# The main PSUM banks as four tiles in place of two tiles of two banks, with new tables for the first and the last batches

## The chip, the cores and the metric

The kernel runs on one core of one Trainium2 chip. The metric is the device time of one execution in microseconds (us), the median of three runs. A core has five engines that work side by side and meet at semaphores: TensorE (PE; its weight loads are shown as PEld), VectorE (DVE), ScalarE (ACT), GpSimd (POOL) and SyncE (SP, which here issues the DMAs).

## The reference

The input is attention-like data of 8 batches, 8 heads, 576 positions and 64 features per head. Each batch goes through a decaying linear attention (retention) and then a gated feed-forward block with a spatial mixing matrix.

```python
scores = scale * (q @ k^T)
ret = (scores * Dmat) @ v                    # Dmat: gamma_h ** (i - j) for i >= j, else 0
x = ret, heads side by side                  # (8, 576, 512)
h = max(x @ w_in, 0); u, v = halves of h     # (8, 576, 512) each
v_n = (v - mean) / sqrt(var + 1e-6)          # over the last axis
v_s = w_spatial @ v_n + b_spatial            # over the 576 positions
out = (u * v_s) @ w_out
```

## The kernel before

Everything is unrolled and runs in an order written out by hand. The kernel is a set of generators ("chains"), one for each small piece of work, such as a product, its eviction from PSUM and the additions that follow. Three strings, `ORDER` (lines 41 to 87), `STEADY` (lines 88 to 110) and `LAST` (lines 111 to 127), list the chains by name; each time a name stands there, that chain is advanced by one step. Each engine receives its instructions in the order in which the steps are traced (`keep_in_program_order`), so that every engine's queue is in order, and only semaphore waits shift the queues against each other.

`ORDER` is played once: it loads and splits the weights (`w`), does batches 0 and 1, and starts on batches 2 and 3. `STEADY` is played five times, for a = 2 to 6, and each time finishes batch a while it works on the retention of batches a+1 and a+2. `LAST` is played once for batch 7. Names in the tables that the text below speaks of: `w` splits a piece of a weight into a high and a low part, and its two letters say whether POOL (p) or DVE (v) does the second and the last step; `p` updates the retention state; `A` makes summed weight blocks; `W` and `Y` are one block product each (6 matmuls for one PSUM bank), followed by one or two additions on DVE or a copy on ACT; `y`, `X`, `F`, `U`, `V`, `G` are whole products (12 to 14 matmuls); `v` with a last number of 4 handles the remaining 64 rows.

PSUM has eight banks. Four belong to the retention (`r0` and `r1`, two banks each). The other four serve all the main products. They are two tiles, `m0` and `m1`, of two banks each. The string `BANKS` (line 128) gives the bank of each next product, digit k being half k % 2 of tile k // 2: banks 0 and 1 lie in `m0`, banks 2 and 3 in `m1`. The waits are put in by the framework from the accesses of each tile. In the program before, a matmul that starts in bank 0 waits for every earlier read of `m0`, thus also for a read of bank 1, its neighbour; and a read of bank 0 waits for the matmuls that were traced ahead of it into bank 1. The other tile's banks put no such wait on it. `weight` (from line 376) also uses a bank, as scratch for integer operations on DVE.

`pair_chain` (from line 900) and its table name `Q` take a whole two-bank tile at once; no table names `Q`.

All the engines' instructions are recorded through one helper, so that the profile gives line 175 for nearly all of them; they are told apart by their tiles: `m<-slot,wout` is a matmul into a main bank, from activations and the output weight, `o<-m,o` on DVE reads a main bank and adds it to a result.

Of the kernel before, what the change touches and what calls it, by code (L numbers as in the profile page):

```python
# [46 lines left out]
    w.1.0.vp g.0.2 w.0.0.vp p.0.2.pp v.0.0 p.0.1.pp w.1.2.vv w.1.1.vp b.0.1 w.0.0.vp p.0.2.pp p.0.2.pp d.1.0 v.0.0 S
    d.1.0 w.1.3.vp g.0.2 b.0.2 w.1.2.vv w.0.0.vp v.0.1 w.0.1.vp w.0.1.vp w.0.0.vp b.0.2 k.0.3.p t.0.p b.0.2 w.0.2.vp
    d.1.1 p.0.2.pp p.0.2.pp b.0.2 w.0.1.vp q.0.3.v g.0.3 s.0.p p.0.3.pp p.0.3.pp S d.1.1 t.0.p p.0.3.pp b.0.2 v.0.1
    w.0.0.vp w.0.2.vp d.1.0 p.0.3.pp v.0.1 b.0.2 S t.0.p g.0.3 v.0.0 v.0.0 v.0.1 w.0.1.vp w.0.2.vp v.0.1 b.0.3 v.0.0  # L50
    w.0.1.vp w.0.2.vp v.0.1 g.1.0 s.1.p d.1.1 g.1.0 b.0.3 s.2.p v.0.1 b.0.3 b.0.3 e.0.p D.0.3 v.0.0 v.0.2 b.0.3
    v.0.1 w.0.1.vp w.0.0.vp v.0.2 k.1.0.p v.0.2 s.1.p S v.0.2 b.0.3 p.1.0.vp v.0.0 e.0.p w.0.2.vp k.1.1.p w.0.3.vv
    v.0.0 q.1.0.p v.0.1 w.0.2.vp p.1.0.vp v.0.4 s.5.p s.2.p v.0.4 q.1.1.p w.0.3.vv v.0.0 v.0.4 v.0.1 p.1.0.vp v.0.3
    v.0.3 D.2.1 e.0.p p.1.0.vp v.0.4 v.0.0 s.3.p s.3.p d.1.2 v.0.3 p.1.0.vp v.0.2 b.1.0 w.0.3.vv b.1.0 v.0.2 g.1.1
    p.1.1.pv b.1.0 v.0.2 D.2.0 d.1.2 d.1.2 w.0.3.vv v.0.4 b.1.0 w.0.3.vv s.0.p D.2.2 U.1 v.0.2 T.1 s.4.p s.5.p v.0.4
    d.1.3 s.4.p p.1.1.pv v.0.3 v.0.2 g.1.1 v.0.4 U.1 v.0.3 p.1.1.pv v.0.4 k.1.2.p v.0.2 b.1.0 v.0.4 U.0 V.0.0 b.1.0
    U.0 p.1.1.pv V.0.0 v.0.3 v.0.4 w.0.2.vp b.1.1 b.1.1 v.0.3 g.1.2 V.0.0 b.1.1 w.0.1.vp b.1.1 p.1.2.vp v.0.4 v.0.4
    v.0.3 q.1.2.p v.0.3 v.0.4 v.0.3 w.0.3.vv d.2.0 v.1.0 p.1.1.pv v.1.0 p.1.2.vp w.0.3.vv v.1.0 w.2.0.pv p.1.2.vp
    g.1.2 b.1.1 v.1.0 V.0.0 V.0.0 w.2.0.pv w.2.1.vp v.1.0 d.2.0 p.1.2.vp b.1.1 d.1.3 V.0.0 V.1.0 b.1.2 b.1.2
    w.2.0.pv w.2.1.vp V.0.3 D.2.3 V.0.3 g.1.3 V.1.0 t.1.p q.1.3.p w.2.1.vp b.1.2 b.1.2 V.1.2 w.2.0.pv w.2.1.vp  # L60
    w.2.1.vp p.1.2.vp d.1.3 V.0.1 V.0.1 w.2.0.pv w.2.2.vp k.1.3.v w.2.0.pv v.1.0 A.0.0.v A.0.1.p t.1.p V.1.2
# [24 lines left out]
    K.2.4.vv F.1.1.1 F.1.1.2
# [25 lines left out]
    v.a.4 v.a.4 W.a.0.1 v.a.4 W.a.0.2.p W.a.1.1 W.a.1.1 W.a.0.2.p W.a.0.1 W.a.0.6 W.a.0.6 W.a.0.7 W.a.0.2.p v.a.4  # L112
    W.a.0.7 W.a.0.5 W.a.0.5 W.a.0.5 W.a.0.3 W.a.1.2.p v.a.4 W.a.0.4 W.a.0.3 W.a.0.4 W.a.1.2.p v.a.2 W.a.1.6 W.a.1.6
    v.a.0 W.a.1.7 v.a.2 W.a.1.7 W.a.1.2.p v.a.0 W.a.1.5 v.a.4 W.a.1.4 v.a.2 v.a.0 W.a.1.5 W.a.1.3 N.a.0 W.a.1.5
    N.a.0 v.a.4 W.a.1.4 Y.a.1.0.6 v.a.0 W.a.1.3 v.a.4 v.a.2 v.a.0 v.a.3 v.a.2 Y.a.1.0.1 Y.a.1.0.1 v.a.4 Y.a.1.0.2.v
    Y.a.1.0.2.v Y.a.1.0.6 v.a.1 v.a.3 Y.a.1.0.7 Y.a.1.0.7 Y.a.1.0.5 Y.a.1.0.2.v Y.a.1.0.4 Y.a.1.1.1 v.a.1 v.a.1
    Y.a.1.0.5 Y.a.1.0.5 v.a.3 N.a.1 Y.a.1.0.3 Y.a.1.0.4 N.a.1 Y.a.1.1.2.p v.a.4 v.a.4 v.a.3 Y.a.1.0.3 v.a.4 v.a.3
    v.a.1 Y.a.1.1.6 Y.a.1.1.2.p Y.a.1.1.7 v.a.1 Y.a.1.1.5 Y.a.1.1.1 Y.a.1.1.6 Y.a.1.1.7 Y.a.1.1.2.p X.a.1.2
    Y.a.1.1.5 X.a.1.2 Y.a.1.1.3 X.a.1.3 Y.a.1.1.5 X.a.0.1 X.a.1.1 Y.a.1.1.3 X.a.1.3 X.a.0.1 X.a.0.0 X.a.1.1
    r.a.1.1.p X.a.1.0 X.a.0.0 r.a.1.1.p r.a.0.0.v X.a.0.2 r.a.0.0.v X.a.1.0 J.a.5.vv X.a.0.2 J.a.5.vv Y.a.1.1.4  # L120
    X.a.0.3 Y.a.2.0.1 J.a.7.pp J.a.7.pp J.a.7.pp Y.a.1.1.4 J.a.6.vv X.a.0.3 J.a.6.vv r.a.1.0.v J.a.6.vv r.a.1.0.v
    J.a.4.vp J.a.5.vv Y.a.2.0.1 J.a.4.vp Y.a.2.0.6 J.a.4.vp Y.a.2.0.2.v Y.a.2.0.6 Y.a.2.0.5 Y.a.2.0.7 Y.a.2.0.2.v
    Y.a.2.0.4 Y.a.2.0.2.v Y.a.2.0.7 Y.a.2.0.2.v Y.a.2.0.5 Y.a.2.0.4 Y.a.2.0.5 Y.a.2.1.1 Y.a.2.0.3 Y.a.2.1.6
# [8 lines left out]
def retention_gmlp(ctx, tc, qkv, tails, w_in, w_sp, b_sp, w_out, amask, qscale, kdec, sdec, out):  # L132
# [58 lines left out]
    idle = wsp[0][:, 0, :512]  # L191
    ve.memset(idle.bitcast(F32), 0.0)

    banks = itertools.chain(BANKS, itertools.cycle("0123"))

    bank_pairs = [ps_m.tile([P, 2, 512], F32, name=f"m{i}") for i in range(2)]

    def bank():
        k = int(next(banks))
        return bank_pairs[k // 2][:, k % 2]  # L200

    def pair():
        k = next(banks)
        return bank_pairs["ab".index(k)]
# [873 lines left out]
```

## Time and profile before

| | before |
|---|---|
| median of three runs | 633.07 us (632.54 to 635.56) |
| time of the profiled execution | 634.95 us |
| its span, first to last instruction | 633.2 us |
| PE matmul busy | 523.5 us (83%) |
| PE weight loads busy | 478.5 us (76%) |
| DVE busy | 390.3 us (62%) |
| ACT busy | 257.0 us (41%) |
| POOL busy | 185.2 us (29%) |

A busy share is the time in which an engine had an instruction in hand; idle time stands with the instruction that ended it, and with what that instruction waited for (its releaser). By the issue of the last store of batch 1 (197.5 us) and of batch 6 (563.4 us), the run falls into three stretches: the first table to about 197.5 us, five steady passes to 563.4 us, and the last batch.

### The profile page before, as it was taken

To read this page: it belongs to the slowest core of one execution; us is meant where nothing else is said; L and a number is where in the kernel's file an instruction comes from. 1 tells how busy PE (TensorE), PEld (TensorE's weight loads), DVE (VectorE), ACT (ScalarE), POOL (GpSimd) and SP (SyncE) were. 2 spreads that over 40 slices of the span, in tenths; PEclk is the share of its full clock that TensorE was granted. 3 is DMA by queue.
4 is the path that set the end of the run, shared out by engine and by line. 5 is a ranking of instruction groups with operands and counts; after the bars stand their busy time and mean duration, and the time that the engine had idled before them with its cause. 6 is when DMAs were issued, how large, how long until landed. Compare 5 with 4: busy or idle time off the path is not lost.

```text
span 633.2 us, 16971 instructions
## 1 busy us (share of the span) xinstructions
PE 523.5 (83%) x7304; PEld 478.5 (76%) x7304; DVE 390.3 (62%) x810; ACT 257.0 (41%) x572; POOL 185.2 (29%) x178
## 2 busy tenths in 40 slices
PE   2876977879999898778988989898887889887875
PEld 2665876769998788767987879777876779777775
DVE  4885565845447646676568655776476665665453
ACT  2363423433234723337234551446232471347320
POOL 1767226634042113221332212231133112210121
PEclk9988999989999999999999999999999999999999
DMA  8973410103334410152103511153101600010002
GB/s 312 393 224 107 130 56 3 55 31 121 101 110 133 141 52 1 46 186 89 52 2 101 185 35 51 46 178 98 51 2 55 196 3 2 20 57 0 2 2 75
DMA packets 29805, 55.40 MB, mean 87 GB/s; under 512 B 3233, under 2 KB 15649, under 8 KB 29474
## 3 DMA queue, kind: packets, MB, share of 16 engines
q1 hardware_dynamic: 29730, 54.32, 26.2%
q8 instruction: 57, 0.93, 0.6%
q14 instruction: 18, 0.15, 0.1%
HBM read 44.87 MB, written 9.44 MB: 86 GB/s over the span
## 4 chain that ended last, share of the span: by engine, by line
PE 53%; DVE 16%; ACT 7%; issue 3%; DVEq 0%; ACTq 0%
PE m L175 47%; DVE u L175 6%; PE r L175 5%; DVE o L175 3%; DVE slot L175 3%; ACT u L175 2%; ACT vt L175 1%; ACT slot L175 1%; ACT vn L175 1%; ACT o L175 1%; DVE sms L175 1%; DVE x L175 1%; DVE vt L175 1%; DVE vn L175 0%; DVE at L175 0%
## 5 line engine op out<-in xcount | busy, mean ns | idle before, releaser
L175 PE MATMUL m<-wsp,vn 128*128 128x288 f32 x768 | 114.3, 297 | 10.6 <-DVE u L175 4.2
L175 DVE TENSOR_TENSOR u<-m,u 128x256 f32<-128x256 f32 (+1 forms) x144 | 61.0, 438 | 97.7 <-PE m L175 81.8
L175 PEld LDWEIGHTS m<-wsp,vn 128*128 128x128 f32 x768 | 105.6, 188 | 13.4 <-DVE u L175 3.8
L175 PE MATMUL m<-slot,win 128*128 128x288 f32 x480 | 76.3, 305 | 23.3 <-DVE u L175 5.7
L175 PEld LDWEIGHTS m<-slot,win 128*128 128x128 f32 x480 | 67.2, 192 | 28.5 <-DVE u L175 6.6
L175 PE MATMUL m<-slot,wout 128*128 128x288 f32 x480 | 74.4, 304 | 11.7 <-DVE o L175 7.7
L175 PEld LDWEIGHTS m<-slot,wout 128*128 128x128 f32 x480 | 67.2, 192 | 15.5 <-DVE o L175 10.3
L175 ACT CAST slot<-u 128x576 fp32r<-128x576 f32 x46 | 30.7, 673 | 113.3 <-DVE u L175 107.1
L175 POOL TENSOR_TENSOR u<-u 128x256 f32<-128x256 f32 (+2 forms) x24 | 22.2, 925 | 168.9 <-DVE u L175 155.4
L175 PE MATMUL m<-slot,quarter 128*128 128x288 f32 x360 | 59.1, 303 | 13.9 <-DVE u L175 6.3
L175 PEld LDWEIGHTS m<-slot,quarter 128*128 128x128 f32 x360 | 50.0, 188 | 18.3 <-DVE u L175 8.5
L175 PE MATMUL m<-win,slot 128*128 128x256 f32 (+1 forms) x312 | 58.1, 329 | 3.7 <-DVE u L175 1.0
L175 PEld LDWEIGHTS m<-win,slot 128*128 128x128 f32 x312 | 46.9, 193 | 11.6 <-DVE u L175 1.6
L175 PE MATMUL m<-quarter,slot 128*128 128x256 f32 x288 | 41.7, 290 | 6.4 <-DVE u L175 5.0
L175 POOL TENSOR_TENSOR slot<-u,slot 128x576 fp32r<-128x576 f32 x20 | 29.7, 1483 | 55.8 <-ACT slot L175 55.8
L175 ACT COPY u<-m 128x288 f32<-128x288 f32 (+1 forms) x60 | 22.1, 390 | 54.5 <-PE m L175 45.7
L175 PEld LDWEIGHTS m<-quarter,slot 128*128 128x128 f32 x288 | 36.4, 188 | 10.1 <-DVE u L175 7.1
L175 ACT CAST slot<-x 128x576 fp32r<-128x576 f32 (+1 forms) x43 | 28.0, 672 | 27.6 <-DVE x L175 15.7
L175 ACT COPY o<-m 128x288 f32<-128x288 f32 (+1 forms) x42 | 18.1, 431 | 52.0 <-PE m L175 41.8
L175 DVE TENSOR_TENSOR o<-m,o 128x288 f32<-128x288 f32 x66 | 27.8, 450 | 18.2 <-PE m L175 15.5
L175 DVE SCALAR_TENSOR_TENSOR u<-u,m 128x288 f32<-128x288 f32 x48 | 21.4, 448 | 24.9 <-PE m L175 24.6
L175 PE MATMUL r<-qsc,sh 64*64 64x64 f32 x512 | 28.8, 231 | 1.5 <-DVE sh L175 0.7
(149 smaller groups left out, 936.4 us busy)
## 6 DMA issues: line engine op xcount, KB each, us to landing
qk<-in_qkv SPq DMA_DIRECT2D x30, 512.0 KB, 4.3
out<-o SPq DMA_DIRECT2D x58, 144.0 KB, 1.9
kn<-in_qkv SPq DMA_DIRECT2D x30, 256.0 KB, 4.5
vv<-in_qkv SPq DMA_DIRECT2D x30, 256.0 KB, 4.7
tail<-in_tails SPq DMA_DIRECT2D x8, 384.0 KB, 3.1
lent_slot<-in_w_in SPq DMA_DIRECT2D x4, 512.0 KB, 7.4
raw<-in_w_in SPq DMA_DIRECT2D x4, 512.0 KB, 9.6
raw<-in_w_out SPq DMA_DIRECT2D x4, 512.0 KB, 5.2
```

The costliest lines, as they stand in the source:

```text
L175: ins = op(*args, **kw)
```

## The change

The four main banks become four tiles of one bank each. A digit of `BANKS` is then the tile itself. `pair_chain`, `pair` and the name `Q` go.

`STEADY` is unchanged. `BANKS` is new throughout; in the five passes of `STEADY` the new digits are the old ones with 2 and 3 exchanged, so that two products share a bank after the change exactly where they did before it. `ORDER` has the same 673 steps in another order, and `LAST` the same 174. In `ORDER`, 32 steps that were on DVE go to POOL and 23 go from POOL to DVE; in `LAST` a few steps change between the two as well.

```diff
 ORDER = """
-    D.1.3 w.1.3.vp m w.1.3.vp d.0.0 D.1.1 c.k g.0.0 c.a d.0.0 k.0.0.p w.1.1.vp w.1.3.vp w.1.1.vp d.0.0 w.1.3.vp
-    w.1.1.vp D.1.0 c.q g.0.0 D.1.2 w.1.1.vp c.d w.1.3.vp p.0.0.pp w.1.0.vp d.0.1 q.0.0.v p.0.0.pp d.0.1 w.1.0.vp
...
+    D.1.0 d.0.0 g.0.0 w.1.0.vv D.1.2 c.k c.a w.1.0.vv d.0.0 k.0.0.p w.1.0.vv d.0.0 w.1.2.vv D.1.3 w.1.2.vv w.1.3.vp
+    g.0.0 w.1.2.vv m w.1.2.vv c.q w.1.0.vv q.0.0.v p.0.0.pv p.0.0.pv b.0.0 b.0.0 D.1.1 c.d p.0.0.pv w.1.0.vv d.0.1
...
 LAST = """
-    v.a.4 v.a.4 W.a.0.1 v.a.4 W.a.0.2.p W.a.1.1 W.a.1.1 W.a.0.2.p W.a.0.1 W.a.0.6 W.a.0.6 W.a.0.7 W.a.0.2.p v.a.4
...
+    W.a.0.2.p W.a.0.1 W.a.0.6 W.a.0.2.p W.a.0.7 W.a.0.1 W.a.0.6 W.a.0.2.p W.a.0.5 W.a.0.3 W.a.0.7 W.a.0.4 W.a.0.5
...
-    banks = itertools.chain(BANKS, itertools.cycle("0123"))
-
-    bank_pairs = [ps_m.tile([P, 2, 512], F32, name=f"m{i}") for i in range(2)]
+    banks = itertools.chain((int(k) for k in BANKS), itertools.cycle(range(4)))
+
+    bank_tiles = [ps_m.tile([P, 512], F32, name=f"m{i}") for i in range(4)]
 
     def bank():
-        k = int(next(banks))
-        return bank_pairs[k // 2][:, k % 2]
-
-    def pair():
-        k = next(banks)
-        return bank_pairs["ab".index(k)]
+        return bank_tiles[next(banks)]
...
-    def pair_chain(b, kind, i, eng=po):
...
-        "Q": lambda b, kind, i, how="p": pair_chain(int(b), int(kind), int(i), on(how)),
```

## Rows read from the trace of the kernel before

**Rows 1.** The page: busy time of each engine, and of its 40 slices of the span (15.8 us each) the lines of PE and of TensorE's granted clock, in tenths.

```profile
PE 523.5 (83%) x7304; PEld 478.5 (76%) x7304; DVE 390.3 (62%) x810; ACT 257.0 (41%) x572; POOL 185.2 (29%) x178
...
PE   2876977879999898778988989898887889887875
...
PEclk9988999989999999999999999999999999999999
```

**Rows 2.** Busy time by stretch: first table in three parts, five steady passes, last batch. Columns: stretch and its length, then busy time (and instructions) of PE, PEld, DVE, ACT and POOL, granted clock, share of the DMA engines, GB/s.

```profile
0.00:60.00 60.00, 36.74 (x788) 29.17 (x788) 42.87 (x86) 26.70 (x54) 34.14 (x40) 0.97 0.80 274
60.00:120.00 60.00, 49.94 (x681) 44.40 (x682) 38.71 (x84) 22.73 (x48) 23.62 (x21) 0.97 0.20 63
120.00:197.50 77.50, 70.91 (x1004) 67.21 (x1003) 43.89 (x82) 29.41 (x70) 30.30 (x24) 0.98 0.26 81
197.50:563.40 365.90, 313.09 (x4466) 288.72 (x4465) 231.62 (x490) 154.20 (x349) 88.18 (x87) 1.00 0.23 75
563.40:633.20 69.80, 52.82 (x372) 49.01 (x370) 33.19 (x72) 24.00 (x54) 8.99 (x8) 0.98 0.07 23
```

**Rows 3.** Who PE waited for in the steady stretch (197.5 to 563.4 us): the waiting engine and the tile it writes, what it waited for, us in total, times, longest.

```profile
PE m L175 <- DVE u L175: 18.5, 22, 1.7
PE m L175 <- DVE o L175: 17.8, 15, 2.4
PE m L175 <- ACT u L175: 4.5, 8, 0.8
PE r L175 <- ACT r L175: 3.3, 4, 1.1
PE m L175 <- ACT vt L175: 2.4, 3, 1.1
PE m L175 <- ACT r L175: 1.8, 2, 0.9
PE r L175 <- DVE st L175: 1.7, 2, 0.8
PE m L175 <- ACT o L175: 1.2, 3, 0.5
PE m L175 <- DVE vt L175: 1.1, 2, 0.5
PE m L175 <- DVE slot L175: 0.2, 1, 0.2
```

**Rows 4.** PE's timeline at the same step of four steady passes: the group of `Y.a.2.1.1` that follows the group of `Y.a.2.0.4`, in the passes for batches 2, 3, 4 and 5. Columns: start, us, engine, line, operation, out<-in, count, and in brackets the idle time before it and its releaser; equal neighbours are merged (x12 is both groups, back to back).

```profile
258.96 1.07 PE L175 MATMUL m<-slot,wout 128*128 128x288 f32 x6
262.45 1.06 PE L175 MATMUL m<-slot,wout 128*128 128x288 f32 x6 [2.43 <-DVE o L175]
263.36 2.55 PE L175 MATMUL m<-slot,quarter 128*128 128x288 f32 x18
...
332.77 1.07 PE L175 MATMUL m<-slot,wout 128*128 128x288 f32 x6
334.54 1.06 PE L175 MATMUL m<-slot,wout 128*128 128x288 f32 x6 [0.70 <-DVE o L175]
...
403.75 1.87 PE L175 MATMUL m<-slot,wout 128*128 128x288 f32 x12
...
481.60 1.07 PE L175 MATMUL m<-slot,wout 128*128 128x288 f32 x6 [2.43 <-DVE o L175]
```

**Rows 5.** DVE's timeline around the first of these four (pass for batch 2), same columns.

```profile
255.80 0.45 DVE L175 TENSOR_TENSOR o<-m,o 128x288 f32<-128x288 f32 x1
...
260.06 0.95 DVE L175 TENSOR_TENSOR o<-m,o 128x288 f32<-128x288 f32 x2 [0.97 <-PE m L175]
...
261.59 0.81 DVE L175 TENSOR_TENSOR o<-m,o 128x288 f32<-128x288 f32 x2
```

**Rows 6.** Busy time in three consecutive stretches, each from one step of `STEADY` to the same step of the next pass (columns as in rows 2).

```profile
240.75:315.54 74.79, 62.57 (x916) 58.50 (x917) 46.81 (x98) 30.90 (x70) 20.41 (x20) 1.00 0.24 79
315.54:386.75 71.21, 63.44 (x919) 58.35 (x917) 45.24 (x98) 30.19 (x69) 15.69 (x17) 1.00 0.26 83
386.75:459.88 73.13, 64.40 (x917) 58.56 (x917) 48.99 (x103) 31.69 (x71) 18.55 (x18) 1.00 0.26 81
```

**Rows 7.** PE's timeline: the first and the last of the 47 waits of the steady stretch, then the first and the last of 14 in the first table, then the first and the last of 7 in the last batch, in which a group of matmuls into a main bank was released by a read of the neighbouring bank of its tile.

```profile
201.65 0.98 PE L175 MATMUL m<-quarter,slot 128*128 128x256 f32 x6 [0.59 <-DVE u L175]
...
563.03 1.20 PE L175 MATMUL m<-win,xt 128*128 128x512 f32 x4 [1.70 <-DVE o L175]
...
26.41 0.97 PE L175 MATMUL m<-win,slot 128*128 128x512 f32 x3 [0.79 <-DVE m L175]
...
197.13 0.74 PE L175 MATMUL m<-win,slot 128*128 128x256 f32 x4 [0.27 <-ACT o L175]
...
571.39 0.98 PE L175 MATMUL m<-win,slot 128*128 128x256 f32 x6 [0.20 <-DVE u L175]
...
627.12 1.06 PE L175 MATMUL m<-slot,slot 128*128 128x288 f32 x6 [0.19 <-DVE o L175]
```

**Rows 8.** Groups of instructions in the first table (0 to 197.5 us): busy us, mean ns of one | idle before them.

```profile
L175 POOL TENSOR_TENSOR win<-f,win 128x512 fp32r<-128x512 f32 x4 | 5.1, 1284 | 0.7 <-ACT win L175 0.7
L175 POOL TENSOR_TENSOR x<-win,win 128x512 f32<-128x512 f32 x6 | 8.9, 1494 | 12.9 <-issue 10.8 <-DVE quarter L175 2.0
L175 DVE TENSOR_TENSOR win<-f,win 128x512 fp32r<-128x512 f32 x1 | 0.7, 679 | 0.0
L175 DVE TENSOR_TENSOR x<-win,win 128x512 f32<-128x512 f32 x2 | 1.3, 668 | 0.0
L175 DVE TENSOR_TENSOR x<-wout,wout 128x512 f32<-128x512 f32 x3 | 3.4, 1131 | 0.1
```

More of the change, by code (lines that the diff above doesn't have):

```diff
@@ L47 @@
[L47 to L61, printed above, removed]
@@ new lines @@
+    F.0.0.1 e.1.p e.1.p v.1.4 A.1.3 w.2.3.pp w.2.3.pp v.1.4 e.1.p q.2.0.v v.1.4 w.2.3.pp d.2.2 P.1.0.p F.0.0.2
+    P.1.1.p v.1.2 A.1.12.v A.1.7 v.1.4 y.1.2.0 w.2.3.pp y.1.0.0 p.2.0.pp v.1.4 y.1.2.0 p.2.0.pp p.2.0.pp v.1.2
+    A.1.13.v y.1.3.0 y.1.0.0 b.2.0 p.2.0.pp w.2.3.pp k.2.1.v v.1.4 b.2.0 F.0.0.3 P.1.0.p d.2.1 A.1.4.p v.1.2 g.2.1
+    A.1.14 v.1.2 y.1.3.0 v.1.4 p.2.1.vp F.0.0.3 A.2.1.v F.0.0.2 b.2.0 b.2.0 v.1.2 A.1.15.p d.2.2 v.1.4 v.1.2 P.1.1.p
+    A.2.5.p p.2.1.vp y.1.3.1 v.1.4 y.1.2.1 q.2.2.v v.1.4 g.2.1 F.0.0.0 d.2.2 q.2.1.v y.1.2.1 v.1.4 d.2.3 A.1.10
@@ new lines @@
+    y.1.0.1 A.2.0.v p.2.1.vp F.0.0.0 A.1.8.v v.1.3 y.1.3.1 A.2.2.v v.1.3 F.0.1.1 p.2.1.vp F.0.0.3 v.1.3 A.2.6.v
+    y.1.0.1 v.1.3 v.1.4 d.2.3 v.1.4 A.2.12.p y.1.1.1 F.0.1.1 v.1.3 v.1.3 v.1.3 F.0.0.0 p.2.1.vp v.1.3 y.1.1.1
+    F.0.1.3 v.1.3 F.0.1.3 A.2.13.v A.1.11.p F.0.1.2 A.2.7 A.2.14 v.1.3 F.0.1.0 A.2.15.v k.2.3.v A.2.3 F.0.1.0
+    X.1.1.2 F.0.1.2 F.0.1.0 A.2.4.p X.1.0.2 X.1.1.0 A.2.8.v X.1.1.2 y.1.1.0 k.2.2.v X.1.0.2 b.2.0 b.2.1 g.2.2 b.2.1
+    p.2.2.vp b.2.1 X.1.1.2 b.2.1 X.1.0.2 X.1.0.2 d.3.0 X.1.0.1 p.2.2.vp X.1.1.2 b.2.1 p.2.2.vp d.2.3 X.1.0.0 y.1.1.0
@@ new lines @@
+    W.a.0.5 W.a.0.3 W.a.0.4 W.a.1.6 W.a.1.1 v.a.2 W.a.1.7 v.a.0 v.a.2 v.a.4 W.a.1.1 v.a.0 v.a.4 v.a.4 v.a.2 v.a.0
+    N.a.0 W.a.1.6 W.a.1.2.v W.a.1.2.v v.a.4 W.a.1.7 N.a.0 W.a.1.5 W.a.1.4 W.a.1.2.v v.a.4 v.a.4 v.a.2 W.a.1.5
+    W.a.1.4 Y.a.1.0.1 W.a.1.5 v.a.0 v.a.4 W.a.1.3 v.a.1 v.a.4 v.a.0 Y.a.1.0.6 W.a.1.3 v.a.2 Y.a.1.0.2.p Y.a.1.0.1
+    Y.a.1.0.7 Y.a.1.0.6 Y.a.1.0.5 v.a.1 v.a.3 Y.a.1.0.7 Y.a.1.0.2.p v.a.3 v.a.1 Y.a.1.0.4 v.a.3 Y.a.1.0.3
+    Y.a.1.0.2.p Y.a.1.0.5 v.a.4 N.a.1 Y.a.1.0.4 N.a.1 Y.a.1.1.2.v Y.a.1.0.5 v.a.3 v.a.1 Y.a.1.0.3 v.a.3 v.a.1
@@ new lines @@
+    Y.a.1.1.2.v Y.a.1.1.1 Y.a.1.1.1 Y.a.1.1.6 v.a.4 Y.a.1.1.5 v.a.4 Y.a.1.1.7 Y.a.1.1.6 Y.a.1.1.3 v.a.4 Y.a.1.1.2.v
+    Y.a.1.1.7 X.a.0.0 X.a.0.1 Y.a.1.1.5 X.a.0.0 Y.a.1.1.5 X.a.1.0 X.a.1.1 X.a.1.0 Y.a.1.1.3 X.a.0.1 X.a.1.3
+    r.a.0.0.p X.a.1.2 Y.a.1.1.4 X.a.1.1 X.a.1.3 r.a.0.0.p J.a.5.vv X.a.1.2 J.a.7.vp r.a.1.1.v J.a.7.vp X.a.0.2
+    r.a.1.1.v X.a.0.3 J.a.6.vp J.a.5.vv J.a.6.vp X.a.0.2 J.a.7.vp Y.a.1.1.4 Y.a.2.0.1 Y.a.2.0.7 X.a.0.3 r.a.1.0.v
+    r.a.1.0.v Y.a.2.0.1 J.a.6.vp Y.a.2.0.6 Y.a.2.0.2.v J.a.5.vv Y.a.2.0.6 Y.a.2.0.5 J.a.4.vp Y.a.2.0.7 Y.a.2.0.2.v
@@ L898, in product_chain @@
         yield from combined(i, ps, u[:, m, lo], u[:, 2 + m, lo], u[:, m, hi], u[:, 2 + m, hi], eng)
-    def pair_chain(b, kind, i, eng=po):
-        u = u_tile_of()
-        lo, hi = slice(0, HALF), slice(HALF, S)
-        if kind == 1:
-            c11, c12, c21, c22 = u[:, 0:2, lo], u[:, 0:2, hi], u[:, 2:4, lo], u[:, 2:4, hi]
-        else:
-            r = results()
-            c11, c12, c21, c22 = r[:, 0:2], r[:, 2:4], u[:, 0:2, hi], u[:, 2:4, hi]
-        ps = pair()[:, :, :HALF]
-        for m in range(2):
-            product(kind, i, m, ps[:, m])
-            yield
-        yield from combined(i, ps, c11, c12, c21, c22, eng)
-        if kind == 2 and i in (2, 5, 4, 3):
-            t, half_of, src = {2: (0, 0, c11), 5: (1, 1, c22), 4: (0, 1, c21), 3: (1, 0, c12)}[i]
-            dma(out[b, half_of * 256:(half_of + 1) * 256, t * HALF:(t + 1) * HALF].rearrange("(a p) n -> p a n", a=2), src)
-            yield
     def single_chain(b, kind, m, i, eng=po):
```

80 lines of the change are left out of this document (37 added, 43 removed).

## The prediction, made before the change was run

> **What bounds the kernel now.** The page comes first [rows 1]: PE is the busiest engine with 523.5 of 633.2 us, DVE follows with 390.3, and nothing else is near. PE's slices are low only in the first tenth of the span and at its end; in between they stand at 7 to 9 and never settle at 9. The granted clock is full almost everywhere, so PE's missing time is idle time, not a slow clock. The stretches [rows 2] say how much and where: 39.9 us idle in the first table (197.50 less 36.74, 49.94 and 70.91), 52.8 in the five steady passes (365.90 less 313.09), 17.0 in the last batch (69.80 less 52.82). The steady passes are the longest stretch and repeat, so who ends PE's idle time there is what I read next [rows 3]. The rows add up to 52.5 us, and all but 5.0 of it (the two `PE r` rows) is a wait of a matmul into a main bank, nearly always for DVE or ACT, which read or combine such a bank: 47.5 us.
>
> A wait for a read of a main bank is honest when the bank is the one about to be overwritten, and a by-product of the two-bank tile when it is the neighbour. The rows give the time, `ORDER`, `STEADY` and `BANKS` give the banks, and one step shows how they go together. In the pass for batch 2, `Y.2.2.1.1` goes to bank 0 and starts at 262.45 after 2.43 us of idle time [rows 4]. Its releaser is the second addition of the pair that DVE starts at 261.59 and ends at 262.40 [rows 5], which reads bank 1, for `Y.2.2.0.5`. Bank 0 itself was last read by the addition of 255.80, over at 256.25 [rows 5]. PE was held for the neighbour. The same step in the next passes has 0.70 us (bank 1, held by a read of bank 0), nothing at all (bank 3, back to back with the group before it), and 2.43 again [rows 4]. The order of all engines is the same in these passes; only the bank numbers rotate, with a period of three passes. So three like passes, step to step, take 74.79, 71.21 and 73.13 us [rows 6]. Bank numbers alone, through the tile, move a pass by 3.6 us.
>
> Done for every wait, this gives 47 waits of the steady stretch, 14 of the first table and 7 of the last batch that were ended by the neighbour bank [rows 7]. Each counted only up to the next thing that its group needed anyway (a read of its own bank, its operands, or PE's own previous group), they hold PE for 39.9, 14.2 and 5.6 us. The same kind of wait holds DVE and ACT: an eviction waits for matmuls that were traced ahead of it into the neighbour. I give these no price of their own, since they count only through PE.
>
> **The four tiles, steady passes.** `STEADY` doesn't change and the digits of `BANKS` are a renaming, so the honest waits stay as they are and the 47 go. What is late next? At 262.45: the group could start when the one before it ends, 258.96 + 1.07 = 260.03, which is 2.42 us earlier. Six matmuls take 0.91 us from start to start (262.45 to 263.36 [rows 4]). The group after it goes to bank 2, which the first of the two additions of 260.06 has read by some 260.5; the third goes to bank 3, which the first of the two of 261.59 reads until about 262.04 [rows 5]. It was to start at 260.03 + 1.7 = 261.7 and waits until 262.1, so 0.4 of the 2.43 comes back as an honest wait, and 2.0, a share of 0.84, is kept. I take that share for all: 39.9 x 0.84 = 33.5 us. A lower end comes from rows 6: the three passes hold 10.4, 5.0 and 5.8 us of such waits, and a line through the three points has a slope of 0.56, thus 22 us; three points, one of them out of line, are weak evidence, and evictions that are free sooner are not in them, so I stay near the hand-worked step. The upper end is all of PE's idle time here, 52.
>
> **The first table.** The 14 waits give 14.2 x 0.84 = 12 us. The new order is another matter. Its first steps still fetch one piece of weight and then the first chunk, so I leave the start as it is. On balance 32 - 23 = 9 more steps run on POOL. A split costs 1.28 us there and 0.68 on DVE, a sum 1.49 against 0.67 [rows 8]; so POOL gains some 13 us of work and DVE loses 6. In the first 60 us DVE is busy for 42.87 and POOL for 34.14, later both less [rows 2]: neither is full on the average, and a chain that goes through POOL gets 0.6 to 0.8 us longer a step. I take 2 us off, thus 10 us. The bounds are wide, as no row shows the new order: if all 32 steps sat on the path, 32 x 0.7 = 22 us would be lost against the 12, thus -10; if it were as tight as the steady passes, PE's idle time after 60 us (10.1 + 6.6) and some of the 23.3 before it would go, thus +25.
>
> On this point a rule speaks against the change. The same sum of two weight blocks on DVE takes 668 ns in one group of rows and 1131 in another [rows 8], so something beside it can slow it. The Trainium skill (SBUF — State Buffer, section "Who interferes with whom") says that DVE and GpSimd share a pair of ports under an exclusive lock and that a DVE instruction with two SBUF inputs contends with a GpSimd instruction that reads SBUF; the two groups agree with it, though they don't prove it. By it, more work on POOL would also make DVE's sums longer, up to 0.46 us each.
>
> **The last batch.** Seven waits: 5.6 x 0.84 = 4.7 us. A table made for this batch alone needs no room for a next one; I add 1.3 for it, thus 6. The bounds are 0 and the 12 us that PE is idle here ahead of the closing 5 us (its last group starts at 627.12 [rows 7], after which DVE and the store end the run).
>
> **Removing `pair_chain`** and `Q` removes nothing that runs: no table names it.
>
> **The sum.** 33.5 + 10 + 6 = 49.5 us. The span of 633.2 becomes 583.7; the profiled execution has 1.75 us around its span (634.95), which gives 585.4, and it stands 1.88 above the median of the runs, which gives 583.5. I predict 583.5 us.
>
> **Rivals.** *Honest waits take over.* As PE runs ahead, it meets the reads of its own bank and the operands that DVE has still to make. For it: the slope of 0.56, and that DVE is busy for 45 to 49 us a pass [rows 6], which is some 72% of a 65 us pass. Against it: the step of rows 4 goes without any idle time in the pass whose banks allow it. With the slope, 59.7 x 0.56 = 33 us and no gain from the tables: 600; with half of that, 616. I put it at 600 to 618.
>
> *PE becomes the bound.* All of the 52 us of the steady stretch go, 20 of the first table and 12 of the last: 549; with nine tenths of it, 557. For it: only 47.5 - 43.5 = 4 us of the main banks' waits in the steady stretch were not ended by a neighbour (the 47 hold 43.5 us in full). Against it: stalls never vanish altogether in an order that was fixed for other waits. Matmul rows overlap, and the Trainium skill (Perfetto Trace Analysis, section "Identifying the Most-Contended Engine") holds the busy share of weight loads to be the better measure of PE's headroom; by it the floor of the steady stretch would be 288.7 and not 313.1 us [rows 2], an estimate from its rule and this trace that only moves this rival lower.
>
> *Nothing changes.* If the framework still tied neighbours together, the new banks would be the old ones under other names, and the steady passes would take the same 366 us: 630 to 636.
>
> *Slower.* The first table puts POOL on the path: 32 steps, each 0.6 to 0.8 us longer than on DVE [rows 8], 19 to 26 us, and DVE's sums beside them up to 0.46 us longer. It decides only where the waits give back less than that, as they would if the steady passes kept their length: 633 + 22 - 5 = 650. For it: POOL is already busy in 57% of the first 60 us [rows 2]. Against it: 39.9 us of waits in a stretch whose order is untouched.
>
> **How the numbers follow.** Forecast (570 to 600): 0.60. Honest waits take over (600 to 618): 0.20. PE the bound (549 to 570): 0.13. Nothing changes: 0.03. Slower: 0.04. To hold 8 in 10 the range takes about half of each neighbouring case: 562 to 608. Some 0.5% is what a measurement of this kernel can tell from no change; faster by more than that is 0.93, within it 0.03, slower by more 0.04.
>
> **What the profile after would show.** If I am right on the tiles, PE's waits in the steady stretch fall from 52.5 to 15 to 20 us, and the passes become equally long, some 66 us each, since banks no longer matter through their tile. At the step of rows 4 no pass shows more than some 0.5 us. Unequal passes would mean that neighbours are still tied. Passes of 69 us or more, with as many waits for DVE as now but on their own banks, would mean the first rival. For the first table, batch 1's last store, now issued at 197.5 us, should come at about 187; if it comes later than 197, the new order costs more than the waits gave. From batch 6's last store to the end there are now 69.8 us, and 64 are expected. A POOL that ends more of DVE's or PE's waits in the first 120 us would bear out the slower rival's mechanism.

## The result and the profile after

The kernel after takes 529.78 us, the median of four runs (529.33 to 531.02), beside 633.14 us for the kernel before in the same runs: a ratio of 0.8365, 95% interval 0.8338 to 0.8391. The time is 16% shorter. The forecast of 583.5 us had the right sign and a little less than half of the size (49.5 us less, measured 103.4), and the range of 562 to 608 does not hold the result. The profiled execution, the slowest of the four, took 531.02 us with a span of 529.2 us. Executions that ran in a slower state, at a lower clock, are left out of the ratios and comparisons below; of the kernel with both halves of the tie put back that leaves one of two.

First the page of the kernel after: busy time, and the slices of PE and of the granted clock (13.2 us each).

```profile
PE 498.8 (94%) x7304; PEld 473.9 (90%) x7304; DVE 387.4 (73%) x803; ACT 255.1 (48%) x572; POOL 197.2 (37%) x185
...
PE   1698999999998999999999999999999999989995
...
PEclk9999999999998999999999999999999999999998
```

From the fifth slice nearly to the end PE's slices stand at 9, with an 8 here and there, where they moved between 7 and 9 before [rows 1]. The busy time of PE fell by 25 us although it runs the same 7304 matmuls. That row is the first hint of what my sum missed.

The stretches follow, cut at the issue of the last store of batch 1 and of batch 6 as before; columns as in rows 2.

```profile
0.00:60.00 60.00, 42.91 (x940) 35.57 (x941) 47.54 (x102) 31.68 (x64) 40.80 (x43) 1.00 0.81 273
60.00:120.00 60.00, 60.00 (x775) 56.55 (x775) 50.47 (x90) 27.85 (x61) 43.10 (x36) 1.00 0.30 95
120.00:167.90 47.90, 44.08 (x704) 42.89 (x702) 24.05 (x51) 19.02 (x45) 14.71 (x13) 1.00 0.28 91
167.90:471.60 303.70, 301.98 (x4522) 290.83 (x4523) 232.83 (x490) 153.06 (x348) 89.97 (x89) 0.99 0.28 90
471.60:529.20 57.60, 49.85 (x368) 48.08 (x366) 32.56 (x73) 23.52 (x54) 8.58 (x7) 0.98 0.08 29
```

Against [rows 2], the first table goes from 197.5 to 167.9 us (29.6 less), the steady stretch from 365.9 to 303.7 (62.2 less), the last batch from 69.8 to 57.6 (12.2 less). Together that is the whole difference of the spans, 104.0. In the steady stretch PE is idle for 1.7 us (303.70 less 301.98), where it had been 52.8. The other 11.1 of the 62.2 are busy time that went: 313.1 before, 302.0 now, for the same passes (the cut counts 56 matmuls more now, x4522 beside x4466). In the first table the clock column rose as well: [rows 2] has 0.97, 0.97 and 0.98 there, and all three parts now have 1.00.

Who PE waited for in the steady stretch of the kernel after; these are all the rows of the view, beside the ten of [rows 3].

```profile
PE r L174 <- DVE at L174: 2.5, 1, 2.5
PE m L174 <- POOL slot L174: 1.2, 1, 1.2
PE r L174 <- ACT r L174: 0.3, 1, 0.3
```

No group of matmuls waits for a read of a main bank any more, neither its neighbour's nor its own. The single wait of 2.5 us ends at 168 us, at the seam between the first table and the first pass, and most of it lies ahead of the cut at 167.90.

The step of [rows 4], in the same four passes after the change (PE's timeline, x12 is both groups back to back):

```profile
222.21 1.86 PE L174 MATMUL m<-slot,wout 128*128 128x288 f32 x12
...
282.27 1.86 PE L174 MATMUL m<-slot,wout 128*128 128x288 f32 x12
...
342.34 1.86 PE L174 MATMUL m<-slot,wout 128*128 128x288 f32 x12
...
402.40 1.86 PE L174 MATMUL m<-slot,wout 128*128 128x288 f32 x12
```

The idle time of 2.43, 0.70, 0 and 2.43 us is gone in every pass, and from step to step the passes take 60.06, 60.07 and 60.06 us, where [rows 6] had 74.79, 71.21 and 73.13. Bank numbers no longer show in the time.

DVE's longest waits in the steady stretch, before the change and after it, were the other half of the matter. The kernel before (197.5 to 563.4 us):

```profile
DVE u L175 <- PE m L175: 86.1, 72, 4.6
DVE o L175 <- PE m L175: 12.7, 11, 2.1
```

and the kernel after (167.9 to 471.6 us):

```profile
DVE u L174 <- PE m L174: 44.0, 65, 5.1
...
DVE o L174 <- PE m L174: 0.8, 2, 0.4
```

DVE waited 54 us less for matmuls. A part of that follows from PE being earlier. The experiments tell the rest.

### The profile page after: what moved, and what is told of

It reads as the page before. It is cut to its first block, busy times and chain, and to the rows that moved or that the text cites. A ratio compares the mean times of both kernels' runs of the same rounds, so it can differ in the third digit from the quotient of the medians.

```text
span 529.2 us, 16959 instructions
## 1 busy us (share of the span) xinstructions
PE 498.8 (94%) x7304; PEld 473.9 (90%) x7304; DVE 387.4 (73%) x803; ACT 255.1 (48%) x572; POOL 197.2 (37%) x185
## 5 line engine op out<-in xcount | busy, mean ns | idle before, releaser
L174 DVE TENSOR_TENSOR u<-m,u 128x256 f32<-128x256 f32 (+1 forms) x144 | 60.6, 436 | 31.6 <-PE m L174 21.0
L174 POOL TENSOR_TENSOR u<-u 128x256 f32<-128x256 f32 (+3 forms) x23 | 21.4, 931 | 135.9 <-DVE u L174 124.1
L174 PE MATMUL m<-slot,win 128*128 128x288 f32 x480 | 71.3, 297 | 0.6 <-DVE u L174 0.6
L174 PE MATMUL m<-slot,wout 128*128 128x288 f32 x480 | 71.0, 297 | 0.0
L174 PEld LDWEIGHTS m<-slot,win 128*128 128x128 f32 x480 | 65.8, 188 | 1.7 <-DVE u L174 0.9
L174 PEld LDWEIGHTS m<-slot,wout 128*128 128x128 f32 x480 | 65.7, 188 | 0.7
L174 PE MATMUL m<-win,slot 128*128 128x256 f32 (+1 forms) x312 | 55.7, 321 | 2.6 <-issue 1.3
L174 PE MATMUL m<-slot,quarter 128*128 128x288 f32 x360 | 57.4, 300 | 0.0
L174 POOL TENSOR_TENSOR slot<-u,slot 128x576 fp32r<-128x576 f32 x21 | 32.0, 1525 | 50.9 <-ACT slot L174 50.9
L174 PE MATMUL m<-quarter,slot 128*128 128x256 f32 x288 | 39.9, 286 | 0.6 <-DVE slot L174 0.3
L174 PE MATMUL r<-qk 64*64 64x64 f32 x960 | 21.6, 230 | 8.5 <-DMA qk<-in_qkv 6.0
```

Of the source, the lines that this page charges most:

```text
L174: ins = op(*args, **kw)
```

## The experiments

The question is where some 54 us more than forecast came from. Theory A: the gain is all in the tiles, in the steady passes first of all, and the new tables have little part in it. Its rival: the new first and last tables carry what I missed. Within A, theory A1 holds that only PE's waits for reads of a neighbour count, as the prediction had it; theory A2 that the mirror wait (a read held by matmuls into the neighbour) has a price of its own. Ratios are to the kernel before, run on the same chip, with a 95% interval.

**The tiles alone, with all tables of before.**

```diff
-    bank_pairs = [ps_m.tile([P, 2, 512], F32, name=f"m{i}") for i in range(2)]
+    bank_tiles = [ps_m.tile([P, 512], F32, name=f"m{i}") for i in range(4)]
...
-        return bank_pairs[k // 2][:, k % 2]
+        return bank_tiles[int(next(banks))]
```

> The kernel before with its own tables and its own bank digits; only the two tiles of two banks become four tiles of one. Theory A (the tie between neighbouring banks is nearly the whole loss, the new tables are second): the five steady passes, whose order is that of the kernel after, take 61 us each as there (305 in all against 366), the first table falls from 197.5 to some 175 to 185, the last batch from 70 to some 62; in all 540 to 555. Theory B (the tables found anew carry as much as the tiles, as 583 had been expected from the tiles): 570 to 590, with steady passes of 66 us.

523.38 us (523.34 to 524.07), ratio 0.8236 (0.8195 to 0.8277): the whole gain and 6 us more. That is beyond the 540 to 555 that theory A was given, on the side away from its rival. Windows of this run, with the seams at its own last stores of batches 1 and 6:

```profile
0.00:60.00 60.00, 45.04 (x964) 37.50 (x965) 49.39 (x108) 32.56 (x66) 40.01 (x45) 1.00 0.84 290
60.00:120.00 60.00, 60.00 (x774) 56.59 (x773) 48.20 (x97) 28.68 (x63) 32.99 (x26) 1.00 0.23 75
...
164.80:463.00 298.20, 297.82 (x4472) 286.94 (x4471) 230.14 (x490) 153.22 (x349) 88.68 (x87) 1.00 0.28 92
463.00:521.50 58.50, 49.49 (x362) 47.25 (x360) 33.63 (x72) 23.82 (x54) 8.91 (x8) 0.99 0.08 28
```

First table 32.7 us less than before, steady stretch 67.7 less, last batch 11.3 less. PE is idle for 0.4 us of 298.2.

**The tables alone, on two tiles of two.** The same edit undone in the kernel after.

```diff
-    bank_tiles = [ps_m.tile([P, 512], F32, name=f"m{i}") for i in range(4)]
+    bank_pairs = [ps_m.tile([P, 2, 512], F32, name=f"m{i}") for i in range(2)]
...
-        return bank_tiles[next(banks)]
+        k = next(banks)
+        return bank_pairs[k // 2][:, k % 2]
```

> The kernel after with its new tables and digits, but the four banks again as two tiles of two. Theory A: the steady passes are as long as in the kernel before, some 73 us each, and the new first and last tables, which were not made for tied banks, give nothing or lose: 620 to 655. Theory B: the new tables keep their part, 585 to 605.

646.74 us (644.50 to 650.44), ratio 1.0179 (1.0123 to 1.0235): some 2% slower than before. So A holds and its rival falls. The tiles are worth 117 us under the new tables (646.74 less 529.78), and the new tables cost some 11 us without the tiles and 6 with them.

**PE's half of the tie put back.** The kernel after, with an explicit dependency: a matmul into a main bank waits for the last read of its neighbour by DVE and by ACT, as it did in the tile of two banks. Reads are not held.

```diff
+                for k in own:
+                    for who in (("dve", "act") if mine == "pe" else ()):
+                        other = last.get((k ^ 1, who))
+                        if other is not None:
+                            tc.add_manual_dep(ins.ins, other, ...)
+                    last[k, mine] = ins.ins.name
```

> The kernel after, with one half of the tie put back as explicit dependencies: each matmul into a main bank also waits for the earlier reads (by DVE and ACT) of the neighbouring bank; reads stay free. Theory A1 (the idle time that PE spent behind such reads was the loss, as the prediction counted it, 0.84 of 60 us): 575 to 585, with steady passes of 68 us. Theory A2 (the two directions of the tie work on each other: a read that is held by the neighbour's matmuls comes later and then holds PE; one direction alone costs much less): 540 to 560, with steady passes of 62 to 66 us.

570.20 us, ratio 0.8969 (0.8911 to 0.9027). This lies between the two ranges, 575 to 585 and 540 to 560, and bears out neither theory by itself.

**The reads' half put back.** The same code, but a read waits for the last matmul into the neighbour, and matmuls are not held.

```diff
-                    for who in (("dve", "act") if mine == "pe" else ()):
+                    for who in (("pe",) if mine != "pe" else ()):
```

> The kernel after, with the other half of the tie put back: each read of a main bank (by DVE and ACT) also waits for the matmuls traced ahead of it into the neighbouring bank; PE's matmuls stay free. Theory A1 (such waits count only through PE's own holds, so they cost next to nothing by themselves): 530 to 536. Theory A2: some cost of its own, since late reads come back as waits of PE for its own bank, 540 to 570.

578.19 us, ratio 0.9095 (0.9029 to 0.916). A1, which gave it 530 to 536, falls; the 540 to 570 of A2 were too low as well. Alone, this half costs 48 us (578.19 less 529.78), PE's half 40; by the ratios, each against the kernel before beside it, 46 and 38. The reads' half loses more than the other in the first table and in the last batch (183.2 against 173.5 us, 67.0 against 60.6), and less in the steady stretch. The steady stretch of the three kernels, one row each: PE's half, the reads' half, and both (the tables alone, on two tiles of two).

```profile
173.50:507.30 333.80, 311.45 (x4519) 292.08 (x4520) 234.90 (x490) 153.43 (x348) 90.02 (x89) 0.99 0.25 82
```

```profile
183.20:511.10 327.90, 311.17 (x4523) 293.64 (x4524) 234.56 (x490) 153.22 (x348) 90.92 (x89) 0.99 0.26 83
```

```profile
203.90:577.40 373.50, 320.90 (x4517) 296.03 (x4518) 231.80 (x490) 154.25 (x348) 90.26 (x89) 0.99 0.22 73
```

Against 303.7 us of the kernel after, PE's half adds 30.1, the reads' half 24.2, and both 69.8, which is 15.5 more than their sum. The execution behind the last row was the slowest of its four (650.44, median 646.74), so some of the 15.5 can be its own; the medians of the whole runs have the same sign, 117 against 40 and 48. My reading, which no run parts from others: a read that is held keeps its own bank longer, and the matmuls that are held for reads then wait longer too. About a third of each cost stands in PE's busy time and not in its idle time: of the 30.1 us, 9.5 (311.45 less 301.98), of the 24.2, 9.2.

The two halves look different in the waits of PE. PE's half, the two longest rows on main banks (173.5 to 507.3 us):

```profile
PE m L175 <- DVE u L175: 9.6, 16, 0.9
PE m L175 <- DVE o L175: 7.7, 11, 1.7
```

and the reads' half, the longest row and the longest on main banks (183.2 to 511.1 us):

```profile
PE r L175 <- ACT r L175: 5.7, 4, 2.2
PE m L175 <- DVE o L175: 2.5, 4, 0.8
```

In the second, no matmul is held for a neighbour. The time reaches PE in many small waits that my count of neighbours could not contain: for the retention's banks, for reads of a bank's own that now come late (that is what a wait of a main bank for `o` or `u` can still be here; 6.5 us in this stretch), and for a few late operands.

**Both halves put back by hand**, to see that the two dependencies are the whole tie.

```diff
-                    for who in (("dve", "act") if mine == "pe" else ()):
+                    for who in (("dve", "act") if mine == "pe" else ("pe",)):
```

> The kernel after with both halves of the tie as explicit dependencies (matmuls wait for reads of the neighbour, reads wait for the neighbour's matmuls). If the two halves together are the tie, 640 to 648, as with the new tables on two tiles (646.7); if only what each half cost alone adds up (40 + 48), 615 to 620.

638.36 us, a single execution, beside 646.74 (644.50 to 650.44) for the tables alone. The two dependencies bring back 108.6 of the 117.0 us, far more than the 89 of a plain sum, which would have given 615 to 620. So they are some nine tenths of the tie; whether the last 8 us have another cause, one execution can't tell.

**One pair tied**, banks 0 and 1 in one tile, 2 and 3 each in its own.

```diff
+    tied = ps_m.tile([P, 2, 512], F32, name="m0")
-    bank_tiles = [ps_m.tile([P, 512], F32, name=f"m{i}") for i in range(4)]
+    bank_tiles = [tied[:, 0], tied[:, 1]] + [ps_m.tile([P, 512], F32, name=f"m{i}") for i in (2, 3)]
```

> The kernel after with banks 0 and 1 as one tile of two and banks 2 and 3 as tiles of their own. If ties cost in proportion, half of the 117 us between the new tables on four tiles and on two: 585 to 592. If PE can go round one tied pair by way of the free banks, less: 545 to 575.

587.26 us, ratio 0.9251 (0.9181 to 0.9321): 57.5 above the kernel after, half of the 117. One tied pair costs half of two.

**The last table alone**, on four tiles with the first table of before.

```diff
 LAST = """
-    v.a.4 v.a.4 W.a.0.1 v.a.4 W.a.0.2.p W.a.1.1 W.a.1.1 W.a.0.2.p W.a.0.1 W.a.0.6 W.a.0.6 W.a.0.7 W.a.0.2.p v.a.4
...
+    W.a.0.2.p W.a.0.1 W.a.0.6 W.a.0.2.p W.a.0.7 W.a.0.1 W.a.0.6 W.a.0.2.p W.a.0.5 W.a.0.3 W.a.0.7 W.a.0.4 W.a.0.5
...
```

> Four tiles, the first table of the kernel before and the last table of the kernel after (digits 2 and 3 exchanged to fit). In the two runs so far the last batch took 58.5 us with the old table (four tiles alone) and 57.6 with the new one. If the new last table is worth what these stretches say, 522 to 523; if it is worth the 6 us that had been expected of tiles and table together, 517; if the old stretch was only longer because of what came before it, no change from 523.4.

523.93 us (522.59 to 525.22), ratio 0.826 (0.8211 to 0.8309), the same as the tiles alone. The closing additions of DVE show why; first with the last table of before, then with the new one.

```profile
514.97 0.46 DVE L175 TENSOR_TENSOR o<-m,o 128x288 f32<-128x288 f32 x1 [1.88 <-PE m L175]
516.63 1.55 DVE L175 TENSOR_TENSOR o<-m,o 128x288 f32<-128x288 f32 x4 [1.20 <-PE m L175]
```

```profile
512.66 0.46 DVE L175 TENSOR_TENSOR o<-m,o 128x288 f32<-128x288 f32 x1 [1.09 <-PE m L175]
515.57 1.81 DVE L175 TENSOR_TENSOR o<-m,o 128x288 f32<-128x288 f32 x4 [2.45 <-POOL u L175]
```

DVE is 2.3 us earlier (514.97 against 512.66), and then the last four additions wait 2.45 us for an addition on POOL. What the table gains on PE it gives back there for the most part: the four additions start 1.1 us earlier and the span is 0.7 us shorter (520.8 against 521.5), too little to show in the medians.

**That wait taken away**, by doing the product whose sum POOL makes before the one after it.

```diff
-    ... Y.a.2.1.7 Y.a.2.1.5 Y.a.2.1.2.p Y.a.2.1.2.p ...
+    ... Y.a.2.1.7 Y.a.2.1.2.p Y.a.2.1.5 Y.a.2.1.2.p ...
```

> Four tiles, old first table, new last table, with the last two products of the run exchanged (Y.a.2.1.2 ahead of Y.a.2.1.5, and their digits with them). In the run with the new last table PE ended at 514.2 us and not at 516.5, but the last four additions on DVE began only at 515.57, when POOL had added what hangs on the last product; with four tiles alone they began at 516.63. If that product is what the end waits for, its copy on ACT and the addition on POOL come 0.8 us earlier, and the run ends 0.7 to 0.8 us earlier than with the new last table: 522.5 to 523. If the end hangs on the stores or on DVE's additions, no change.

> The four tiles alone with the old tables once more, beside the two above on the same chip: 523.4 as before, within 1 us.

523.26 us (ratio 0.8228, 0.8188 to 0.8268), beside 523.86 for the tiles alone on the same chip (0.8239, 0.8199 to 0.8279): no difference that these runs can tell. The copy on ACT and the addition on POOL stay late, and PE waits 0.55 us for DVE in their place. A miss.

**The new first table** costs 7.7 us of span against the tiles alone (529.2 against 521.5; by the medians 6.4). The last batch gives 0.9 back (57.6 against 58.5). PE's timelines show where the rest goes: the scores of batch 3's second chunk start at 168.06 us against 160.98, the step of [rows 4] for batch 2 at 222.21 against 213.66, 8.6 later, and from there on both kernels keep the same distance. PE does 2.1 us less in the first 60 us (42.91 against 45.04), waits 1.5 us ahead of 145.87 for nothing that the profile shows ("issue"), and then comes to a stop at the seam. These are DVE's lines there, PE's, and the clock in steps of 2 us, in the kernel after; PE's lines are followed by the same two groups of the tiles alone.

```profile
166.31 0.76 DVE L174 TENSOR_TENSOR slot<-x,slot 128x576 fp32r<-128x576 f32 x1 [1.81 <-ACT slot L174]
...
167.32 0.68 DVE L174 TENSOR_TENSOR at<-r,am 128x512 f32<-128x512 f32 x1
```

```profile
168.06 1.13 PE L174 MATMUL r<-qk 64*64 64x64 f32 x32 [2.49 <-DVE at L174]
...
174.11 0.69 PE L174 MATMUL r<-vv,kn 64*64 64x64 f32 x32
```

```profile
160.98 0.69 PE L175 MATMUL r<-qk 64*64 64x64 f32 x32
...
165.59 0.69 PE L175 MATMUL r<-vv,kn 64*64 64x64 f32 x32
```

```profile
166.00:168.00 2.00, 0.00 (x0) 0.00 (x0) 1.70 (x4) 1.44 (x4) 1.10 (x2) 0.99 0.21 74
168.00:170.00 2.00, 1.94 (x41) 1.83 (x42) 2.00 (x3) 0.15 (x1) 2.00 (x2) 0.50 0.68 188
170.00:172.00 2.00, 2.00 (x10) 1.62 (x9) 1.40 (x2) 0.00 (x0) 0.19 (x1) 0.65 0.91 273
```

DVE masks the scores of batch 3's first chunk (`at<-r,am`) only after sums of the output weights that wait for ACT, and the second chunk's scores go to the same place in PSUM, so PE stands for 2.49 us. Behind it the clock is granted at 0.50 for 3.4 us: from the scores to the group of `vv,kn` PE takes 6.05 us, and 4.61 with the tiles alone, thus 1.4 more. With 2.1 and 1.5 that makes 7.5 of the 8.6.

*The mask earlier.* The step `g.3.0`, which makes it, ahead of the sums:

```diff
-    F.1.0.1 F.1.1.2 F.1.0.1 F.1.0.1 p.3.0.vv F.1.0.3 R.2.1.0.v F.1.0.0 K.2.5.vv K.2.7.vp ...
+    F.1.0.1 F.1.1.2 F.1.0.1 F.1.0.1 p.3.0.vv F.1.0.3 R.2.1.0.v F.1.0.0 g.3.0 K.2.5.vv K.2.7.vp ...
...
-    F.1.1.2 K.2.4.vv F.1.1.1 K.2.7.vp p.3.0.vv A.2.11.p F.1.1.0 g.3.0 F.1.1.0 ...
+    F.1.1.2 K.2.4.vv F.1.1.1 K.2.7.vp p.3.0.vv A.2.11.p F.1.1.0 F.1.1.0 ...
```

> The kernel after with one step moved: the masking of batch 3's first scores (the second step of g.3.0 in the first table) stands ahead of the first K step and no longer behind the K steps. In the kernel after PE is idle for 2.49 us at 168 us until this step is done on DVE, and its clock stands at half for the 3.4 us that follow. Theory C (this one late step is most of what the new first table costs): 525 to 526. Rival (the new first table has its work in a worse order throughout, and PE would meet the next late thing): 528 to 530.

527.74 us, ratio 0.8313 (0.827 to 0.8356): 2.0 better, not the 4 to 5 that theory C expected, and just under the 528 to 530 of its rival. The wait and its half clock are gone, but another piece of both appeared far ahead of the edit, in PE's timeline and the 2 us windows around 41 us (the clock's windows in the kernel after are at 1.00 there, and its PE waits 1.33 us):

```profile
41.49 4.79 PE L174 MATMUL m<-win,slot 128*128 128x512 f32 x13 [2.21 <-issue]
```

```profile
41.00:43.00 2.00, 1.51 (x4) 1.22 (x5) 1.82 (x9) 1.28 (x3) 1.62 (x2) 0.59 1.00 302
43.00:45.00 2.00, 2.00 (x7) 1.56 (x6) 0.82 (x1) 0.00 (x0) 2.00 (x2) 0.56 0.85 187
```

*The new choice of engine on the old order.* Which steps run on POOL and which on DVE is taken from the new table, the order from the old one, on four tiles; the last table is that of before. Theory C: the cost lies in the order, its rival: in the choice.

```diff
-    w.1.1.vp D.1.0 c.q g.0.0 D.1.2 w.1.1.vp c.d w.1.3.vp p.0.0.pp w.1.0.vp ...
+    w.1.1.vp D.1.0 c.q g.0.0 D.1.2 w.1.1.vp c.d w.1.3.vp p.0.0.pv w.1.0.vv ...
```

> Four tiles with the tables and digits of the kernel before, and of the new first table only the choice between DVE and POOL: every step of the old first table keeps its place, those that differ take the engine of the new one (32 steps to POOL, 23 to DVE). Theory C (PE sets the pace, and only a step that comes late for PE costs; the choice of engine is covered): 522 to 525, like four tiles alone. Rival (the work moved to POOL is what the new first table costs): 527 to 530.

529.54 us, ratio 0.8323 (0.8266 to 0.8379): 5.7 above the 523.86 of the tiles alone on the same chip. The choice by itself costs as much as the whole new table. In the windows of this run PE has 2.8 us less of work done between 60 and 120 us than the row of the tiles alone above, and its two waits there, one of 2.4 us, are for ACT; that is half of the 5.4 us by which the step of [rows 4] comes later (219.03 against 213.66), and the other half isn't traced to a cause:

```profile
60.00:120.00 60.00, 57.19 (x746) 53.07 (x745) 41.69 (x81) 26.42 (x59) 36.99 (x31) 1.00 0.18 60
```

```profile
PE m L175 <- ACT u L175: 2.8, 2, 2.4
```

*The new order with the old choice of engine.* From the last result I turned theory C round: the choice carries the cost, the order next to nothing.

```diff
-    D.1.0 d.0.0 g.0.0 w.1.0.vv D.1.2 c.k c.a w.1.0.vv d.0.0 k.0.0.p w.1.0.vv ...
+    D.1.0 d.0.0 g.0.0 w.1.0.vp D.1.2 c.k c.a w.1.0.vp d.0.0 k.0.0.p w.1.0.vp ...
```

> The new first table's order of steps with the old choice of DVE or POOL for each, four tiles, the new last table. letters_only (old order, new choice) measured 529.54 us, 5.7 above the 523.86 of the tiles alone; the whole new table costs 5.9 to 7.7. Theory C (the choice of engine carries the cost, the order by itself next to nothing): 522 to 526 us. Rival (order and choice are fitted to each other, so that either one alone costs as much as both): 527 to 531 us, with the wait of PE for DVE and its half clock near 168 us still there.

534.47 us (532.10 to 535.75), ratio 0.838 (0.8352 to 0.8408), no better than the kernel after, which is 0.8365. The theory, at 522 to 526, falls. Its rival, order and choice each as costly alone as together, had 527 to 531; the order alone is above that too, so the rival stands in kind and not in size. The wait of 1.5 us for nothing shown is still there (1.48 us at 145.26), and so is the one at the seam, longer:

```profile
168.27 1.13 PE L174 MATMUL r<-qk 64*64 64x64 f32 x32 [3.36 <-DVE at L174]
```

```profile
166.00:168.00 2.00, 0.00 (x0) 0.00 (x0) 2.00 (x3) 0.78 (x2) 0.66 (x1) 0.72 0.17 62
168.00:170.00 2.00, 1.73 (x41) 1.62 (x42) 2.00 (x4) 0.14 (x1) 0.00 (x0) 0.50 0.82 206
170.00:172.00 2.00, 2.00 (x6) 1.61 (x7) 0.82 (x2) 0.01 (x1) 0.00 (x0) 0.50 0.76 265
```

So each half of the new table has a cost of its own, the order in good part at the seam, the choice for a half between 60 and 120 us. Why they don't add up in the kernel after, which pays the first and not the second, stays open.

## Why the prediction was wrong

**Direction and place were right.** The waits for a neighbour's bank were real, they went with the tiles, the steady passes gave most of the gain, and they are now equal. "Nothing changes" (0.03) is out. The change is faster, as 0.93 of the chance said.

**The step that failed first** is "I give these no price of their own, since they count only through PE". The reads held by matmuls into the neighbour cost 24.2 us of the steady stretch by themselves, and 15.5 more together with PE's half. PE's half alone is worth 30.1, close to the 33.5 that I had for the whole. That the two are so close is in part luck: only 20.6 of the 30.1 are idle time (333.80 less 311.45, less the 1.7 of the kernel after), and 9.5 stand in busy time, which I had not counted. So the term that I worked out had about the right size, and a term nearly as large was left out. It does count through PE, but not at the waits that I counted: it comes as late operands, late banks of the retention, and longer reads of a bank's own.

**The share of 0.84** rested on a third group that would wait 0.4 us for a read of its own bank. I took that read at its time in the trace of before, though it was late by the same tie. In the kernel after, the two groups and the three behind them run back to back (222.21 to 226.29), and nothing comes back. The slope of 0.56 from [rows 6], the lower end, pointed the wrong way altogether; passes that differ only in bank numbers have in common all the waits that the numbers don't move, and those don't enter a slope.

**The upper end, "all of PE's idle time"**, 52 us, was no end. The stretch gave 62.2, and 67.7 with the tiles alone, because busy time went too: 313.1 us before, 302.0 after, 297.8 with the tiles alone, which is 70.1, 66.8 and 66.6 ns a matmul (x4466, x4522, x4472) at a clock of 1.00, 0.99 and 1.00. My reading is that matmuls that stall briefly are shown as busy. The row that hardly moves is the weight loads', 288.7, 290.8 and 286.9, or 64.7, 64.3 and 64.2 ns each. The Trainium skill (Perfetto Trace Analysis, section "Identifying the Most-Contended Engine") holds the busy share of weight loads to be a better measure of PE's headroom than that of matmuls, and these three runs agree. I wrote that it "only moves this rival lower" and left the range as it was: with 288.7 in place of 313.1, "PE becomes the bound" begins at 549 less 24, thus 525, and the measured 529.8 lies in it. In kind, this rival is what happened (PE idle for 1.7 us of 303.7). It deserved more than 0.13: only 4 us of the main banks' waits had other causes, as the prediction itself said for it.

**The first table**, forecast at 10 less, came out at 29.6 less, above the bound of 25. The tiles alone give 32.7, so the 12 for its 14 waits were low by the same error as in the steady passes. A second term was put at nothing by "PE's missing time is idle time, not a slow clock": the column of [rows 2] is at 0.97, 0.97 and 0.98 in the three parts, which is up to 5 us of full speed in 197.5 (an estimate: 0.03 of 60, twice, and 0.02 of 77.5), and with the tiles alone it is 1.00 up to 164.8. The 2 us for the new order had the right sign and were too small: 8.6, of which nearly a half falls at the seam to the steady passes (2.5 and 1.4), which I had not thought of as part of that price. **The last batch**, forecast at 6, gave 12.2, just over the bound of 12; the tiles alone give 11.3, and the new last table has no measurable part in it, against my 1.3.

**The slower rival** had a real mechanism. On tied tiles the new tables are slower than the old ones (1.0179), though no run shows that POOL is the reason there, and on four tiles their choice of POOL alone costs 5.7 us. The price of 19 to 26 us was too high, and under a gain of 110 us it could not decide the sign. The sums of weight blocks on DVE did grow longer. The group in the first 164 us of the tiles alone, of the kernel after, and of the new choice on the old order:

```profile
L175 DVE TENSOR_TENSOR x<-win,win 128x512 f32<-128x512 f32 x2 | 1.6, 820 | 0.0
```

```profile
L174 DVE TENSOR_TENSOR x<-win,win 128x512 f32<-128x512 f32 x4 | 3.9, 982 | 0.0
```

```profile
L175 DVE TENSOR_TENSOR x<-win,win 128x512 f32<-128x512 f32 x4 | 6.8, 1710 | 2.1 <-POOL f L175 2.0
```

Beside the 668 ns of [rows 8], that is 0.31 us more in the mean in the kernel after, within my 0.46, and 1.04 with the new choice on the old order, which is more. The Trainium skill (SBUF — State Buffer, section "Who interferes with whom") says that a DVE instruction with two SBUF inputs, as these are, contends with a GpSimd instruction that reads SBUF; the rows agree with its direction, and no run here parts the port from other causes.

**Honest waits take over** (600 to 618) is refuted: no wait of a matmul for its own main bank is left in the steady stretch. No kernel run is better by more than the noise than the tiles alone with every table of before, 523.38 and 523.86 us on two chips; the new tables take back some 6 us of what the tiles give.

## What to carry to other kernels

In this framework the tile is the unit of dependency: where banks of one tile are filled and drained in turn, each needs a tile of its own. Here the tie cost twice, on the writer and on the reader, and more than the sum when both held. To price a false dependency, count both directions, do not take a read's time from a trace in which it was itself held, and take the floor of a PE-bound stretch from the weight loads, since matmul busy time changed here with the waits and the weight loads' hardly did. When a structural edit comes with a new schedule, run the edit with the old schedule too: here the old one was the better.

## What the hardware showed that I had not expected

The granted clock went to 0.50, the lower of its two levels (1.2 GHz), behind a wait of 2.49 us at 168 us and stayed there for 3.4 us; behind 3.36 us of idle time in the run of the new order it stayed low to past 172 us. About as long a wait elsewhere did not do it: in the kernel before PE waits 2.43 us ahead of the group at 262.45 [rows 4], and the clock of that pass is 1.00 [rows 6]. What tells the two apart isn't shown.

The clock column doesn't cover the start of a run. In the kernel after it says 1.00 for the first 60 us, but two groups of 32 like matmuls there have these lines:

```profile
11.71 1.13 PE L174 MATMUL r<-vv,kn 64*64 64x64 f32 x32 [4.62 <-POOL kn L174]
...
31.55 0.64 PE L174 MATMUL r<-at,u 64*64 64x64 f32 x32
```

The first takes 1.13 us, as the group at 168.06 does at a clock of 0.50; the second takes 0.64. The trace's first entry on the clock is at 31.44 us, so the 1.00 ahead of it is no measurement, and by the lines PE runs at half pace until then. With the tiles alone that entry is at 25.36 us, and the 64 matmuls of `r<-lent_wout` take 1.16 us at 28.69, against 1.93 at 29.48 in the kernel after: a part of the 2.1 us that the new first table loses in its first 60 us.

PE also stands for 0.85 to 2.21 us near 38 to 41 us, waiting for nothing that the profile shows ("issue"): 0.85 with the tiles alone, 1.33 in the kernel after, 2.21 with the earlier mask, where the half clock followed. An edit far behind that point came with a longer one, and the cause stays open.
